# Zero products at the head of TensorE's queue, later fetches of two weight groups, and row maxima begun at another time

## The chip, the cores and the metric

The kernel runs on one core of one Trainium2 chip. The metric is the device time of one execution in microseconds (us): a median over runs, and beside it the time of one execution that the hardware profiler recorded. The engines are named as in the profile: PE is TensorE (PEld its weight loads), DVE is VectorE, ACT is ScalarE, POOL is GpSimd, and SP is the queue that only issues transfers.

## The reference, cut to what matters

Sequence length 2048, model width 448, 16 heads of 28, an MLP of width 1792, all in float32.

```
g = sigmoid((x * gate_w).sum(-1))
q, k, v = heads of x @ wqkv
a = softmax(q k^T * 28**-0.5) v, heads joined, @ wo
y = layernorm(x)
b = gelu(y @ w1 + b1) @ w2 + b2
out = g * a + (1 - g) * b
```

## The kernel before

Every operand of a large product is split into a rounded high part and a remainder, and three products are summed in PSUM (high by high, high by low, low by high). Sequence columns go in four chunks of 512.

The kernel has three stretches. In the first, **the head**, one weight block (`wq[0]`), chunk 0 of the transposed input (`xh[0]`, `xl[0]`), two more weight blocks (`wq[3]`, `wq[4]`) and chunks 1 and 2 are fetched through SP into eight buffers and split: the high part by ACT (`x_high`, L102, `mixed_high`, L91), the remainder of x by DVE (`x_low`, L105), that of weights by POOL (`mixed_low`, L95 and L96). `head_split` (L833) issues the splits of one load; the loop at L847 calls it for loads 0 to 10, so for chunk 0, the three weight blocks and chunk 1. Then three full-height accumulations of 11 products each run on PE (L862), one for each of the weight blocks 0, 3 and 4, in the banks 0, 1 and 2. `QK.close` copies a finished bank out (ACT, L282) and stores it in DRAM (`qk`, L286).

In the second stretch, **the strips**, PE's order is written by a planner (`Strips.run`). PE's rows are used as four strips of 32, on which four products run beside each other. The planner keeps a clock of its own, with assumed costs per operation, and issues instructions in the order in which that clock says that they can go: tiles of `QK` (queries and keys), `Val` (values), `Up` and `Down` (the MLP), all with matmuls at L472. Into free strip places it puts the row maxima: `RowMax.one` issues a product of one query tile (`qd`) by 512 keys (`kd`) at L198 and its DVE reduction at L200. There are 1024 of these; those left at the end of the strips are done in the third stretch. PE's own instruction order is what the planner wrote: an instruction that waits holds up all that follow it. Everything else (loads with their `after` times, splits, the loads of keys and queries for the row maxima) is a task with a due time on the planner's clock, and each engine's order is that in which the tasks fell due.

When the last key tile of group 0 is closed, four tasks load the keys and queries of the row maxima through POOL's queue (`rowmax.load_k`, L178; `rowmax.load_q`, L184), and `hot[j]` gives the time at which strip `j` may begin with them:

```
for j in range(4):
    st.at(now + 6.0 + 1.2 * j, lambda j=j: (rowmax.load_k(0, j, nc.gpsimd), ...), pool=1.1)
    st.hot[j] = now + 12.0 + 1.2 * j
```

The value weights `wv` (four loads of 230 KB, L551 on POOL) are due at 32 on that clock, the first ten `w1` blocks at 50. POOL also fetches eight pairs of untransposed input rows (`bxr`) for the layer norm's statistics (DVE, L129 and L130); a buffer is fetched again when its statistics are done.

In the third stretch, **the attention**, a turn makes the scores of 5 or 6 units (L1087), exponentials (ACT, L1090), and value products of whole batches of four units (L1098). While row maxima are owed, a turn has 5 units and up to 3 row maxima (`lone`); later turns have 6. There are 1024 units.

Of the kernel before, what the change touches and what calls it, by code (L numbers as in the profile page):

```python
# [7 lines left out]
F32 = mybir.dt.float32  # L8
F32R = mybir.dt.float32r
# [6 lines left out]
P = 128  # L16
# [6 lines left out]
CH = 512  # L23
# [7 lines left out]
NW = 10  # L31
# [4 lines left out]
def kernel(ctx: ExitStack, tc: tile.TileContext, xt, wqk, wv, wo, xk, w1, b1, w2, b2,  # L36
                          ident_d, sel_d, out):
    nc = tc.nc
# [35 lines left out]
    bk = banks.tile([P, 8, CH], F32, name="bk")  # L74
    ctx.enter_context(tc.manual_schedule())

    p0 = ExitStack()
    px = p0.enter_context(tc.tile_pool(name="px", bufs=1))
    pw = p0.enter_context(tc.tile_pool(name="pw", bufs=5))
    pr = p0.enter_context(tc.tile_pool(name="pr", bufs=1))  # L80
    po = p0.enter_context(tc.tile_pool(name="po", bufs=4))

    lasting = [raws.tile([P, CH], F32, name=f"raw{i}") for i in range(4)]
    passing = [pr.tile([P, CH], F32, name=f"first{i}") for i in range(4)]
    wq, xh, xl = {}, {}, {}

    def four(r):
        return r.rearrange("p (a b) -> p a b", b=P)
# [134 lines left out]
    rowmax = RowMax()  # L223
# [28 lines left out]
    class QK(Piece):  # L252
# [18 lines left out]
        def full(self):  # L271
            w, h, l = wq[self.i], xh[self.c], xl[self.c]
            r = slice(64, 128) if self.i % 2 else slice(0, 64)
            ops = []
            for t in range(3):
                ops += [(w[:, t], h[:, t]), (w[:, t], l[:, t])]
            ops += [(w[:, 3], h[:, 3]), (w[r, 3], l[r, 3])]
            return ops + [(w[:, 4 + t], h[:, t]) for t in range(3)]

        def close(self, st, now):  # L280
            t = po.tile([P, CH], F32, name="qo")
# [106 lines left out]
    class Strips:  # L388


        def __init__(self, tiles):
            self.tiles = tiles
            self.t = [0.0] * 4
            self.visit, self.held = [None] * 4, [None] * 4
            self.feed, self.stat = Feed(self, []), Feed(self, bxr)
            self.live = []
            self.free = {b: 0.0 for b in range(6)}
            self.rm = {6: 0.0, 7: 0.0}
            self.dve = self.act = self.pool = -6.0
            self.clock = self.dma = -6.0  # L400
            self.tasks = []
            self.count = 0
            self.hot = [1e9] * 4
            self.hready, self.yready, self.xready, self.wready, self.w1ready, self.w2ready = {}, {}, {}, {}, {}, {}
            self.vready = 1e9
            self.did = {}
            self.handed = 0

        def use(self, engine, start, cost):
            setattr(self, engine, max(getattr(self, engine), start) + cost)  # L410
# [169 lines left out]
    def want_wq(st, m, **kw):  # L580
        def then(slot, end):
            st.feed.back(slot, end)
            st.wready[m] = end

        def use(r):
            wq[m] = pw.tile([P, 7, P], F32R, name="wq")
            two(st, lambda: mixed_high(wq[m], r), lambda: mixed_low(wq[m], r, m % 2), "pool", 1.6, lambda end: then(r, end))

        st.feed.add(wqk[m], 256, use, **kw)
# [11 lines left out]
    def want_w1(st, f, **kw):  # L601
        def then(slot, end):
            st.feed.back(slot, end)
            st.w1ready[f] = end

        def use(r):
            if f >= NW and w1p[0] is mw0:
                st.later.append(lambda: use(r))
                return
            w1s[f] = w1p[0].tile([P, 7, P], F32R, name=f"w1f{f}")  # L610
            two(st, lambda: mixed_high(w1s[f], r), lambda: mixed_low(w1s[f], r, f % 2), "pool", 1.6, lambda end: then(r, end))

        st.feed.add(w1[f], 256, use, **kw)
# [84 lines left out]
    def done(st, x, now):  # L698
        n = st.did[type(x), x.c]
        if isinstance(x, QK):  # L700
            st.qks.add((x.c, x.i))
            for old, new in ((0, 2), (3, 6)):
                if new not in wq and new not in st.asked and all((c, old) in st.qks for c in range(NC)):
                    st.asked.add(new)
                    want_wq(st, new)
                    st.feed.queue.insert(0, st.feed.queue.pop())
                    st.clock = max(st.clock, now)
                    st.feed.pump()
            if not st.keyed and all((c, m) in st.qks for c in range(NC) for m in (3, 4)):
                st.keyed = True  # L710
                for j in range(4):
                    st.at(now + 6.0 + 1.2 * j, lambda j=j: (rowmax.load_k(0, j, nc.gpsimd), rowmax.load_q(0, j, nc.gpsimd)), pool=1.1)
                    st.at(now + 16.0 + j, lambda j=j: rowmax.load_q(1, j))
                    st.hot[j] = now + 12.0 + 1.2 * j
        elif isinstance(x, Val):
            st.vals += 1
            if st.vals == NT:
                enter_mlp(st, now)
        elif isinstance(x, Up) and n == NF:
            if x.c + 1 < NC:  # L720
                st.go.add(x.c + 1)
                st.clock = max(st.clock, now)
                split_y(st, x.c + 1)
            else:
                early(st, now)

    def enter_mlp(st, now):
        p0.close()
        w1p[0] = w2p[0] = m1.enter_context(tc.tile_pool(name="mw", bufs=1, reuse_waits="tile"))
        mhp.append(m1.enter_context(tc.tile_pool(name="mh", bufs=1, reuse_waits="tile")))  # L730
        hh.extend(mhp[0].tile([P, CH], F32R, name=f"hh{f}") for f in range(NF))
        hl.extend(mhp[0].tile([P, CH], F32R, name=f"hl{f}") for f in range(NF))
        assert not st.stat.out - NT // 2 and all(any(x is y for y in st.feed.slots) for x in passing)
        st.feed.slots = [x for x in st.feed.slots if not any(x is y for y in passing)]
        st.late = True
        st.clock = max(st.clock, now)
        for go in st.later:
            st.at(st.act + 0.6, go)
        for f in range(NF):
            want_w2(st, f)  # L740
        want_ln(st, 1)

    def schedule_head(st):
        st.asked = set()
        st.qks, st.keyed, st.vals = {(0, 0), (0, 3), (0, 4)}, False, 0
        st.xready[1] = st.xready[0] = 0.0
        st.wready.update({0: 0.0, 3: 0.0, 4: 0.0})
        st.late, st.later = False, []
        st.xs, st.wvn, st.stats, st.lns, st.go, st.yn = {}, 0, 0, {}, {0}, {}
        for t in range(4):  # L750
            want_x(st, 3, t)
        for m in (1, 5):
            want_wq(st, m, after=9.0)
        for t in range(4):
            want_wv(st, t, after=32.0)
        for f in range(NW):
            want_w1(st, f, after=50.0)
        st.feed.pump()
        for i in range(NT // 2):
            want_stats(st, i, after=22.0)  # L760
        st.stat.pump()
        st.at(49.0, lambda: nc.sync.dma_start(ones.rearrange("j (a b) -> (j a) b", b=4 * S // P), one_t))
        st.at(50.0, lambda: nc.sync.dma_start(b1s, b1))
        st.at(51.0, lambda: nc.sync.dma_start(sel, sel_d.rearrange("p (j x) -> p j x", x=32)[:, :, 0]))
        st.at(51.5, lambda: nc.sync.dma_start(ident, ident_d))
        st.at(52.0, lambda: nc.sync.dma_start(b2b, b2.partition_broadcast(P)))
# [65 lines left out]
    def head_split(i):  # L832
        key, r = load[i], slots[i % 8]  # L833
        if key[0] == "wq":
            wq[key[1]] = pw.tile([P, 7, P], F32R, name="wq")
            mixed_high(wq[key[1]], r)
            mixed_low(wq[key[1]], r, key[1] % 2)
        else:
            x_high(*key[1:], r)
            x_low(*key[1:], r)  # L840

    loads = [nc.gpsimd]
    strips = Strips([])
# [3 lines left out]
    for i, key in enumerate(load):  # L847
        r = slots[i % 8]
        if key[0] == "wq":
            nc.sync.dma_start(four(r), wqk[key[1]])  # L850
        else:
            nc.sync.dma_start(r, xt[key[2], :, key[1] * CH:(key[1] + 1) * CH])
        if 3 <= i < 14:
            head_split(i - 3)
    strips.feed.slots = slots[7:] + slots[:3]
    schedule_head(strips)
    for b, m in enumerate((0, 3, 4)):
        x = QK(0, m)
        x.bank = b
        ops = x.full()  # L860
        for i, (w, v) in enumerate(ops):
            nc.tensor.matmul(bk[:, b], w, v, start=(i == 0), stop=(i == len(ops) - 1), skip_group_check=True)  # L862
        x.close(strips, -2.4 * (2 - b))
    for i in range(11, len(load)):
        head_split(i)
        strips.use("act", 0.0, 0.65)
        strips.use("dve", 0.0, 0.75)
        strips.feed.back(slots[i % 8], strips.dve + 0.5)
    strips.xready[2] = strips.dve + 0.2
    for c, block in ((1, (3, 4, 0)), (2, (3, 4)), (3, (3, 4)), (2, (0,)), (3, (0,))):  # L870
# [307 lines left out]
```

## Time and profile before

| | us |
|---|---|
| median of 3 runs | 1104.21 |
| lowest and highest | 1100.46, 1105.54 |
| the profiled execution's own time | 1101.01 |
| its span | 1099.1 |
| first product of the strips (L472) | 18.28 from the span's start |
| first product of the attention | 454.72 |

Times in the text are from the span's start. The profiled execution lies 3.2 us under the median and 0.55 us over the lowest run; 1.9 us of it lie outside the span. In the timeline, a row gives the start, the time during which the engine was busy with the merged instructions, the engine, the line, the operation, its operands and the count, and in brackets how long the engine had been idle before, and what released it.

### The profile page before, as it was taken

What the parts mean: (1) busy time and instruction counts of PE and PEld (TensorE: products, weight loads), DVE (VectorE), ACT (ScalarE), POOL (GpSimd) and SP (SyncE); (2) the same over time, 40 slices, a digit from 0 to 9 for tenths busy, and PEclk for the clock granted to TensorE, in tenths of its full rate; (3) what the DMA queues carried; (4) which work ended last, traced back from release to release, by engine and by line L of the source; (5) the groups of instructions that cost most, each with busy time, mean ns of one, the idle gap of its engine ahead of it and who ended that gap; (6) DMA issues with size and microseconds to landing.
All of it is one profiled execution on the core that took longest, in us unless ns stands there. A gap on an engine that the chain in (4) does not pass through costs nothing.

```text
span 1099.1 us, 30449 instructions
## 1 busy us (share of the span) xinstructions
PE 1078.3 (98%) x13153; PEld 727.7 (66%) x13153; DVE 739.7 (67%) x1185; ACT 633.4 (58%) x666; POOL 362.2 (33%) x372
## 2 busy tenths in 40 slices
PE   8989999999999999999999999999999999999998
PEld 5979999999999999744444444444444443454555
DVE  4169999999999999766676775676676664310102
ACT  5324264133042141387787887887887888856672
POOL 3456477535244038321101101310011214434431
PEclk9989999999999999999999999999999999999999
DMA  6685633203000105310000001400002102010211
GB/s 230 203 252 172 212 101 98 92 12 103 36 11 11 37 12 126 111 51 23 20 11 20 24 21 37 104 16 19 16 23 56 48 18 54 24 52 28 69 53 59
DMA packets 47463, 73.15 MB, mean 67 GB/s; under 512 B 13633, under 2 KB 28609, under 8 KB 46417
## 3 DMA queue, kind: packets, MB, share of 16 engines
q1 hardware_dynamic: 33888, 39.11, 12.7%
q0 software_dynamic: 4800, 16.89, 5.6%
q10 hardware_dynamic: 8640, 15.21, 3.9%
q8 instruction: 103, 1.69, 0.7%
q14 instruction: 32, 0.25, 0.1%
HBM read 51.75 MB, written 19.31 MB: 65 GB/s over the span
## 4 chain that ended last, share of the span: by engine, by line
PE 91%; ACT 3%; DMA 2%; issue 1%; POOL 1%; DVE 1%; ACTq 0%; DVEq 0%; SPq 0%; POOLq 0%
PE bk L472 33%; PE bk L1098 21%; PE bk L1087 18%; PE bk L198 14%; ACT p L1090 3%; PE bk L936 1%; PE bk L937 1%; PE bk L938 1%; PE bk L862 1%; DMA qd<-qk 1%; DMA qk<-qo 1%; POOL w1f L95 0%; DVE mx L200 0%; DMA first<-in_xt 0%; PE bk L1114 0%
## 5 line engine op out<-in xcount | busy, mean ns | idle before, releaser
L200 DVE TENSOR_REDUCE mx<-bk 128x1 f32<-128x512 f32 x1024 | 672.1, 689 | 203.2 <-PE bk L198 167.8
L1090 ACT ACTIVATE p<-bk 128x1536 f32<-128x1536 f32 (+1 forms) x393 | 481.6, 1281 | 143.9 <-PE bk L1087 137.7
L198 PE MATMUL bk<-kd,qd 28*128 28x512 f32 x1024 | 447.0, 439 | 6.1 <-DMA qd<-qk 5.2
L198 PEld LDWEIGHTS bk<-kd,qd 28*128 28x128 f32 x1024 | 186.5, 183 | 193.4 <-DVE mx L200 123.5
L472 PE MATMUL bk<-yh,w1f 32*128 32x512 f32 x1568 | 190.2, 393 | 0.1
L472 PE MATMUL bk<-yl,w1f 32*128 32x512 f32 x784 | 165.1, 390 | 0.0
L472 PEld LDWEIGHTS bk<-yh,w1f 32*128 32x128 f32 x1568 | 152.2, 183 | 2.4 <-ACT gb L382 0.8
L472 PE MATMUL bk<-w2h,hh 32*128 32x448 f32 x896 | 141.5, 366 | 0.0
L472 PE MATMUL bk<-w2l,hh 32*128 32x448 f32 x896 | 140.5, 364 | 0.1
L1098 PE MATMUL bk<-p,va 128*32 128x512 f32 x1024 | 131.2, 602 | 0.0
L1098 PE MATMUL bk<-p,vb 128*32 128x512 f32 x1024 | 129.3, 601 | 0.0
L350 POOL TENSOR_TENSOR hl<-h,hh 128x512 fp32r<-128x512 f32 x56 | 72.4, 1306 | 127.5 <-ACT hh L343 76.2
L1087 PE MATMUL bk<-yh,ka 29*128 29x512 f32 x512 | 107.8, 484 | 0.4 <-ACT gb L382 0.4
L472 PEld LDWEIGHTS bk<-yl,w1f 32*128 32x128 f32 x784 | 106.9, 183 | 0.4
L794 POOL CAST yh<-yl 128x512 fp32r<-128x512 f32 x16 | 9.8, 611 | 290.0 <-DMA yl<-qk 180.6
L472 PEld LDWEIGHTS bk<-w2l,hh 32*128 32x128 f32 x896 | 103.0, 183 | 0.7 <-DVE w2l L152 0.4
L472 PEld LDWEIGHTS bk<-w2h,hh 32*128 32x128 f32 x896 | 102.2, 183 | 0.1
L1087 PE MATMUL bk<-yh,kb 29*128 29x512 f32 x512 | 97.5, 477 | 4.1 <-ACT p L1090 4.1
L472 PE MATMUL bk<-w2h,hl 32*128 32x448 f32 x896 | 93.0, 363 | 0.0
L1087 PE MATMUL bk<-yh,la 28*128 28x512 f32 x512 | 88.8, 393 | 0.0
L1087 PE MATMUL bk<-yl,ka 28*128 28x512 f32 x512 | 87.2, 409 | 0.0
L382 ACT ACTIVATE gb<-bk 128x448 f32<-128x448 f32 x16 | 8.7, 544 | 130.2 <-PE bk L472 125.9
(137 smaller groups left out, 1593.7 us busy)
## 6 DMA issues: line engine op xcount, KB each, us to landing
qk<-qo ACTq DMA_DIRECT2D x28, 256.0 KB
raw<-in_xt SPq DMA_DIRECT2D x17, 256.0 KB
vs<-vt ACTq DMA_DIRECT2D x16, 256.0 KB
rc<-rls SPq DMA_DIRECT2D x60, 64.0 KB
bxr<-in_xk POOLq DMA_DIRECT2D x8, 448.0 KB, 6.1
gbs<-gb ACTq DMA_DIRECT2D x16, 224.0 KB
acc<-gbs SPq DMA_DIRECT2D x16, 224.0 KB
out_y<-acc SPq DMA_DIRECT2D x16, 224.0 KB
```

What stands on the lines that cost most here:

```text
L198: nc.tensor.matmul(ps, self.qd[n % 2][r, i * P:(i + 1) * P], self.kd[r, k * 512:(k + 1) * 512], start=True, stop=True)
L200: nc.vector.reduce_max(self.mx[n % 2][:, j, i, k:k + 1], ps, axis=AX)
L350: nc.gpsimd.tensor_sub(hl[f], h, hh[f].bitcast(F32))
L472: mm = nc.tensor.matmul(bk[:, x.bank, :n], a, b, start=x.first, stop=(len(x.rem) == 1 and m == len(ops) - 1), skip_group_check=True)
L794: nc.gpsimd.tensor_copy(h, l.bitcast(F32))
L862: nc.tensor.matmul(bk[:, b], w, v, start=(i == 0), stop=(i == len(ops) - 1), skip_group_check=True)
L936: nc.tensor.matmul(po, h, woh[:, g], start=(g == 0), stop=False, skip_group_check=True)
L937: nc.tensor.matmul(po, h, wol[:, g], start=False, stop=False, skip_group_check=True)
L938: nc.tensor.matmul(po, l, woh[:, g], start=False, stop=(g == NG - 1), skip_group_check=True)
L1087: nc.tensor.matmul(bk[:, i], w[r, ks], q[r], start=(p == 0), stop=(p == 2), skip_group_check=True)
L1090: nc.scalar.activation(t[:, :count], bk[:, first:first + count], AF.Exp, scale=SCALE)
L1098: nc.tensor.matmul(bk[32 * j:32 * j + 32, 7], vg[n // NC][:, k, 32 * j:32 * j + 32], prob.pop(4 * b + j), start=(k == 0), stop=(k == NT - ...
```

## The change

It has four parts.

1. Before the head's products, 512 columns of `kd` are set to zero by DVE. PE multiplies these zeros into bank 7, which holds nothing yet: nine products ahead of the first real one and two more ahead of the products 3, 6 and 9 of the first block (`warm`). The first block now takes the low product of each part directly after the high ones; the other two blocks keep their order.
2. The value weights are due at 42 and the first `w1` blocks at 54 on the planner's clock.
3. The loads of the first keys begin 0.5 earlier after the last key tile's close, they are counted in the planner's model of the transfers, and `hot[j]` is the modelled landing plus 1.5.
4. The planner's clocks of the engines and of the transfers begin at -1 and not at -6; weight blocks have buffers of their own (block 2 in the place of 0, block 6 in that of 3); a late `w1` split waits for the moment at which the MLP's buffers are open.

```
+    PLACE = {2: 0, 6: 3}
...
-            self.dve = self.act = self.pool = -6.0
-            self.clock = self.dma = -6.0
+            self.dve = self.act = self.pool = -1.0
+            self.clock = self.dma = -1.0
...
+            if f >= NW and st.clock < st.opened:
+                st.at(st.opened, lambda: use(r))
+                return
...
+                def first(j):
+                    rowmax.load_k(0, j, nc.gpsimd)
+                    rowmax.load_q(0, j, nc.gpsimd)
+                    st.use("pool", st.clock, 1.1)
+                    st.hot[j] = st.get(st.pool, 290) + 1.5
+
                 for j in range(4):
-                    st.at(now + 6.0 + 1.2 * j, lambda j=j: (rowmax.load_k(0, j, nc.gpsimd), rowmax.load_q(0, j, nc.gpsimd)), pool=1.1)
+                    st.at(now + 5.5 + 1.2 * j, lambda j=j: first(j))
                     st.at(now + 16.0 + j, lambda j=j: rowmax.load_q(1, j))
-                    st.hot[j] = now + 12.0 + 1.2 * j
...
         for t in range(4):
-            want_wv(st, t, after=32.0)
+            want_wv(st, t, after=42.0)
         for f in range(NW):
-            want_w1(st, f, after=50.0)
+            want_w1(st, f, after=54.0)
...
         if 3 <= i < 14:
             head_split(i - 3)
+    nc.vector.memset(rowmax.kd[:, 0:CH].bitcast(F32), 0.0)
+    WARM = {0: 9, 3: 2, 6: 2, 9: 2}
+
+    def warm(n):
+        for _ in range(n):
+            nc.tensor.matmul(bk[:, 7], rowmax.kd[:, 0:P], rowmax.kd[:, 0:CH], start=True, stop=True, skip_group_check=True)
...
     for b, m in enumerate((0, 3, 4)):
         x = QK(0, m)
         x.bank = b
-        ops = x.full()
+        highs, lows = x.full()
+        if b == 0:
+            ops = sum((highs[t] + lows[t:t + 1] for t in range(4)), [])
+        else:
+            ops = sum(highs, []) + lows
         for i, (w, v) in enumerate(ops):
+            if b == 0 and i in WARM:
+                warm(WARM[i])
             nc.tensor.matmul(bk[:, b], w, v, start=(i == 0), stop=(i == len(ops) - 1), skip_group_check=True)
-        x.close(strips, -2.4 * (2 - b))
+        x.close(strips, -2.2 * (2 - b))
     for i in range(11, len(load)):
         head_split(i)
-        strips.use("act", 0.0, 0.65)
-        strips.use("dve", 0.0, 0.75)
+        strips.use("act", 1.0, 0.65)
+        strips.use("dve", 1.8, 0.75)
```

More of the change, by code (lines that the diff above doesn't have):

```diff
@@ L78 @@
     px = p0.enter_context(tc.tile_pool(name="px", bufs=1))
-    pw = p0.enter_context(tc.tile_pool(name="pw", bufs=5))
+    pw = p0.enter_context(tc.tile_pool(name="pw", bufs=1))
     pr = p0.enter_context(tc.tile_pool(name="pr", bufs=1))
@@ L273, in full @@
             r = slice(64, 128) if self.i % 2 else slice(0, 64)
[L274 to L278, printed above, removed]
+            highs = [[(w[:, t], h[:, t]), (w[:, t], l[:, t])] for t in range(3)]
+            highs.append([(w[:, 3], h[:, 3]), (w[r, 3], l[r, 3])])
+            return highs, [(w[:, 4 + t], h[:, t]) for t in range(3)]
         def close(self, st, now):
@@ L585, in use @@
         def use(r):
-            wq[m] = pw.tile([P, 7, P], F32R, name="wq")
+            wq[m] = pw.tile([P, 7, P], F32R, name=f"wq{PLACE.get(m, m)}")
             two(st, lambda: mixed_high(wq[m], r), lambda: mixed_low(wq[m], r, m % 2), "pool", 1.6, lambda end: then(r, end))
@@ L736, in enter_mlp @@
         st.clock = max(st.clock, now)
+        st.opened = st.act + 0.6
         for go in st.later:
-            st.at(st.act + 0.6, go)
+            st.at(st.opened, go)
         for f in range(NF):
@@ L834, in head_split @@
         if key[0] == "wq":
-            wq[key[1]] = pw.tile([P, 7, P], F32R, name="wq")
+            wq[key[1]] = pw.tile([P, 7, P], F32R, name=f"wq{key[1]}")
             mixed_high(wq[key[1]], r)
```

## The prediction

> **What bounds the kernel now.** I read the page's engine shares and chain first, then the list of who waited for whom on PE, then windows around the one long wait, then the timeline of single engines.
>
> ```profile
> PE 1078.3 (98%) x13153; PEld 727.7 (66%) x13153; DVE 739.7 (67%) x1185; ACT 633.4 (58%) x666; POOL 362.2 (33%) x372
> ...
> PE 91%; ACT 3%; DMA 2%; issue 1%; POOL 1%; DVE 1%; ACTq 0%; DVEq 0%; SPq 0%; POOLq 0%
> ```
>
> PE is busy for 98% of the span and makes 91% of the chain. So time is won or lost where PE stands still, where its clock is low, or where its strips are badly filled. PE's list of waits has one long entry behind the head:
>
> ```profile
> PE bk L198 <- DMA qd<-qk: 5.2, 1, 5.2
> ```
>
> (total, times, longest). Windows around it (length, then busy time of PE, PEld, DVE, ACT and POOL with counts, then granted clock, share of the DMA engines, GB/s):
>
> ```profile
> 56.90:62.24 5.34, 0.18 (x3) 0.03 (x2) 0.31 (x1) 0.46 (x1) 3.67 (x5) 0.90 0.95 254
> 62.24:68.04 5.80, 5.80 (x54) 5.07 (x58) 3.27 (x7) 1.55 (x4) 1.28 (x3) 0.50 0.51 150
> ```
>
> PE stands for 5.2 us, and the 5.80 us behind that are granted half the clock. The stop costs 5.2 us and half of 5.8 us, 2.9 us: 8.1 us together.
>
> The head, on PE's timeline:
>
> ```profile
> 9.25 0.79 PE L862 MATMUL bk<-xl,wq 64*128 64x512 f32 x1
> ...
> 12.70 0.63 PE L862 MATMUL bk<-xl,wq 128*128 128x512 f32 x1
> 13.12 0.54 PE L862 MATMUL bk<-xh,wq 128*128 128x512 f32 x1
> ...
> 15.51 0.39 PE L862 MATMUL bk<-xl,wq 128*128 128x512 f32 x1
> 15.74 0.40 PE L862 MATMUL bk<-xh,wq 128*128 128x512 f32 x1
> ...
> 16.66 0.39 PE L862 MATMUL bk<-xh,wq 128*128 128x512 f32 x1
> 16.98 0.50 PE L862 MATMUL bk<-xl,wq 64*128 64x512 f32 x1
> 17.40 0.95 PE L862 MATMUL bk<-xh,wq 128*128 128x512 f32 x3
> 18.28 0.50 PE L472 MATMUL bk<-xh,wq 32*128 32x512 f32 x3
> ```
>
> A product takes 0.42 us from start to start at first (12.70 to 13.12) and 0.23 us later (15.51 to 15.74). The half-height product costs its block 0.28 us more (0.32 and 0.42 us where two steps would be 0.46), and the passage to the strips 0.19 us (17.40 and three steps is 18.09; they begin at 18.28).
>
> **Part 1, the zeros: +11.1 us.** In the source the zeroing of `kd` stands behind the loop that issues the splits of chunk 1, and so it does in DVE's instruction order of the changed program: four small fills, four splits of chunk 0, four of chunk 1, then the zeroing, the thirteenth. PE's first instruction there is a zero product, and it waits for that thirteenth. Nothing of PE stands ahead of it, and all of PE's work stands behind it. DVE before:
>
> ```profile
> 0.84 0.11 DVE L63 MEMSET one_t<- 128x64 f32 x1
> ...
> 12.32 2.15 DVE L105 TENSOR_TENSOR xl<-first,xh 128x512 fp32r<-128x512 f32 x3
> ```
>
> The splits of chunk 1 end at 12.32 + 2.15 = 14.47, and nothing that they wait for comes from PE, so they end there in the changed kernel too. A fill of 128x512 isn't in the trace: at least the 0.11 us of a fill an eighth as long, at most the 0.72 us of a split of its size (2.15 / 3); I take 0.45, between them. PE begins at 15.0. I read this as in-order execution from the rows: the twelve earlier DVE instructions ran in program order. The Trainium skill (TensorE: Matmul & The Clock Gate, Part 1) says the same in so many words, that ACT and DVE are strict FIFO; by it the zeros can't come sooner, and it speaks against this change.
>
> At 15.0 everything that the three blocks read is split, so PE runs through 33 + 15 = 48 products without a wait, the first of them cold. Cold stretches in the trace: 5.8 us behind the stop, and about 4.2 us in the head (steady work from 9.25; the step is down by 13.4). I take 5.0: 11.8 products at 0.425. The other 36.2 at 0.23 are 8.3 us, three half-height products 0.8, the passage 0.2. The strips begin at 15.0 + 5.0 + 8.3 + 1.0 = 29.3 or 29.4, where they began at 18.28: **+11.1 us**. With 4.2 or 5.8 us cold it is 0.4 less or more, with the fill's ends 0.3, so +10.3 to +11.8. Nothing hides this: PE is the bound from there on. The same page (Part 1) has the clock released after about 3.4 us of steady work; that would be 0.8 us less. The trace has longer stretches, and they decide.
>
> ACT's queue has the three copies of finished banks ahead of chunk 2's splits, as before; it moves with PE, and chunk 1 keeps PE busy meanwhile.
>
> **Parts 2 and 3, the stop: -8.1 us.** The chain in order of time, then POOL's queue, then the first row maximum on PE:
>
> ```profile
> 44.32 5.86 DMA qk<-qo
> 53.98 8.12 DMA qd<-qk
> ```
>
> ```profile
> 50.23 0.58 POOL L178 DMA_DIRECT2D kd<-qk  x1
> ...
> 51.88 1.60 POOL L551 DMA_DIRECT2D first<-in_wv  x3
> ...
> 58.28 0.51 POOL L184 DMA_DIRECT2D qd<-qk  x1 [1.55 <-DMA first<-in_wv]
> ```
>
> ```profile
> 55.42 0.46 PE L198 MATMUL bk<-kd,qd 28*128 28x512 f32 x1
> ```
>
> The last key store (44.32) lands at 50.18, the first keys are asked for at 50.23, then come the value weights, and the second query load, issued at 53.98 behind them, takes 8.12 us. It lands at 62.10, and PE stands for it until 62.24. In the changed order all eight loads of keys and queries stand together on POOL, and the value weights behind two `bxr` fetches after them. The changed PE order has 671 strip products ahead of the first row maximum, before 604, which took 55.42 - 18.28 = 37.1 us. At that rate 671 take 41.3 us: the first row maximum comes at 29.4 + 41.3 = 70.7. The last key product has nearly the same place, so the store goes 26.0 us behind the strips' begin, at 55.4, and lands at 61.3. Eight issues of about 0.55 are 4.4 us. Even if the last of them takes the full 8.12 us it lands at 73.8; the first pair, at some 5 to 8 us, at 67 to 70. The order wants the second strip 1.2 us, the third and fourth some 6 and 7 us after the first. So no stop, or a short one, and with it goes the cold stretch: **-8.1 us** (ends -5 and -8.1).
>
> **Strip filling: -1.5 us.** The changed order has 530 row maxima ahead of the attention, before 542. Two windows of the strips:
>
> ```profile
> 140.00:200.00 60.00, 59.81 (x983) 55.79 (x976) 55.23 (x83) 30.78 (x53) 45.18 (x39) 1.00 0.37 107
> 200.00:454.70 254.70, 254.45 (x4411) 245.80 (x4403) 248.80 (x393) 67.89 (x109) 105.85 (x93) 1.00 0.17 48
> ```
>
> A product costs 254.7 / 4411 = 0.058 us, so twelve fewer save 0.7 us. From 140 to 200 it is 0.061 us: 983 x 0.0033 = 3.2 us of unfilled places around the first `Up` and `Down` tiles, which another order can fill or double. I take -0.8 of that, with ends of -3.2 and +3.2. Together -1.5.
>
> **Attention: +1.0 us.** By the program's order there are 159 turns of 5 units, 38 of 6 and one of 1; before 154, 42 and one of 2. The chain shows value batches at a fixed beat:
>
> ```profile
> 517.19 1.86 PE bk L1098 x16
> 528.88 1.85 PE bk L1098 x16
> ...
> 998.52 1.85 PE bk L1098 x16
> 1005.20 1.85 PE bk L1098 x16
> ```
>
> Four turns of 5 are 11.69 us (2.92 each), two turns of 6 are 6.68 us (3.34 each). 5 x 2.92 - 4 x 3.34 = +1.2, less a little for the shorter last turn: +1.0 (ends 0.4 and 2).
>
> **Part 4** only sets due times; its effect is in the counted order. Sum: +11.1 - 8.1 - 1.5 + 1.0 = **+2.5 us**, 1103.5 for an execution like the profiled one. That one lies 3.2 us under the median, so the forecast is 1104.2 + 2.5 = 1106.7 us.
>
> **Rivals.** *The zeros run during the first transfers, as the change means it* (zeroing ahead of the splits, PE warm by 9 us): the first block then ends with chunk 0's last split, near 9.3, and two blocks of 11 x 0.23 + 0.28 = 2.8 us end at about 15.2, so the head is 3 us shorter and the sum -3.1 - 8.1 - 1.5 + 1.0 = -11.7: 1092.5. DVE's order speaks against it: 4%.
>
> *The stop stays*: PE's order still wants a load that hasn't landed. Then the -8.1 is lost and the time is 1114.8, half of it with a stop too short to lower the clock. It decides from a first pair later than 70.7. For it: the DMA engines were 95% busy in that stretch. Against it: 920 KB less stand ahead. 8%.
>
> *The value weights come late*, and PE stops at its first value product instead; the mechanism that makes the kernel slower:
>
> ```profile
> 63.03 0.69 DVE L200 TENSOR_REDUCE mx<-bk 128x1 f32<-128x512 f32 x1 [5.82 <-PE bk L198]
> 63.64 0.62 DVE L129 BATCH_NORM_STATS2 stt<-bxr 128x6 f32<-128x448 f32 x1
> ```
>
> ```profile
> 67.64 2.08 POOL L114 TENSOR_TENSOR wvs<-first,wvs 128x450 fp32r<-128x450 f32 x2 [1.62 <-ACT wvs L110]
> ```
>
> ```profile
> 89.51 0.46 PE L472 MATMUL bk<-wvs,xh 32*128 32x450 f32 x2
> ```
>
> Before, the splits were done by 71, 18 us ahead of use. In the changed POOL order three of them stand behind a `bxr` fetch that waits for statistics, and these stand on DVE behind 13 row maxima: 70.7 + 13 x 0.69 + two statistics of at most 2.5 = 84.7, then 0.7 for the fetch and some 4 for three splits and an issue: 89.4. PE comes to its first value product after about as many products as before, at 89.5 + 11.1 - 8.1 - 1 = 91.5. It decides when POOL is 2 us later than that; each further us costs one, and over some 3 to 5 us the clock falls as well: 1109 to 1116, at the middle 1112. 14%.
>
> **How the numbers follow.** A measurement of this kernel can tell about 0.5%, 5.5 us, from no change. My case has 74%: +2.5 with ends from 1101 to 1112 by its terms and by the spread of the runs; 5% of it lie under -5.5 and 6% over +5.5, by the strip filling and a short wait, 63% between. With the first rival (4%) faster has 9%. The stop that stays (8%), 10 of the 14% of late value weights and those 6% make 24% slower; 67% are within. The range leaves out the first rival and the worst of the stops: 1098.5 to 1114.5.
>
> **What would show it.** Right: PE's first row a zero product near 15.0, waiting for DVE; the strips' begin near 29.4; no wait over 1 us at L199 and a granted clock of 1.00 from 50 to 80; the attention's begin 1 to 3 us later than 454.7. Wrong: a first zero product near 1 or 2 us; a wait on `qd`, `kd` or `wvs` of several us; an attention (454.7 to the end, 644 us) that is longer or shorter by over 2 us.

## The result, and the profile after

| | before | after |
|---|---|---|
| median, us | 1103.83 (4 runs) | 1112.80 (4 runs, 1111.18 to 1113.73) |
| the profiled execution's own time | 1101.01 | 1112.62 |
| its span | 1099.1 | 1110.5 |
| first product of the strips | 18.28 | 29.63 |
| first product of the attention | 454.82 | 464.66 |
| last product | 1093.61 | 1105.02 |

(The 454.72 given for the attention's begin before is that of a row maximum just ahead of its first product.) The changed kernel is slower: the ratio of the times is 1.0092, 95% interval 1.0070 to 1.0114. The forecast was +2.5 us, measured were +9.0 us by the medians and +11.4 us by the two spans (the profiled execution of before lies 2.8 us under its median, that of after 0.2 us). The busy times on the page of after:

```profile
PE 1078.6 (97%) x13168; PEld 727.9 (66%) x13168; DVE 737.4 (66%) x1186; ACT 634.6 (57%) x668; POOL 364.0 (33%) x372
```

PE is busy for 1078.6 us, where it was 1078.3, but the sum hides three differences: it is 1.5 us longer in the head (15 products of zeros), 2.8 us shorter in the strips and 1.6 us longer in the attention. The time in which PE stands grew from 20.8 us (1099.1 - 1078.3) to 31.9 us (1110.5 - 1078.6), and so nearly all of the 11.4 us is to be looked for in the list of PE's waits (total, times, longest):

```profile
PE bk L868 <- DVE kd L863: 14.7, 1, 14.7
...
PE bk L199 <- issue: 2.0, 1, 2.0
PE bk L1108 <- ACT gb L381: 1.8, 1, 1.8
PE bk L471 <- ACT hh L342: 1.3, 1, 1.3
...
PE bk L199 <- DVE mx L201: 0.8, 1, 0.8
PE bk L471 <- ACT gb L381: 0.5, 1, 0.5
PE bk L471 <- ACT qo L281: 0.4, 1, 0.4
```

The long wait for `qd` of before is gone; a wait of 14.7 us for the fill stands at the head, and behind it six of 0.4 to 2.0 us within the strips. PE's timeline of after (start, busy, engine, line, operation):

```profile
14.71 4.21 PE L868 MATMUL bk<-kd 128*128 128x512 f32 x9 [14.71 <-DVE kd L863]
...
20.00 0.64 PE L868 MATMUL bk<-kd 128*128 128x512 f32 x2
20.47 0.39 PE L883 MATMUL bk<-xh,wq 128*128 128x512 f32 x1
20.70 0.40 PE L883 MATMUL bk<-xl,wq 128*128 128x512 f32 x1
...
29.63 0.50 PE L471 MATMUL bk<-xh,wq 32*128 32x512 f32 x3
...
70.20 0.39 PE L199 MATMUL bk<-kd,qd 28*128 28x512 f32 x1
```

DVE's timeline shows the fill directly behind the splits of chunk 1:

```profile
11.97 2.15 DVE L106 TENSOR_TENSOR xl<-first,xh 128x512 fp32r<-128x512 f32 x3
14.18 0.48 DVE L863 MEMSET kd<- 128x512 f32 x1
```

The zeros come 14.71 us after the begin, when all inputs of the three blocks have landed and are split; steps of 0.23 us begin at 20.00; the strips begin at 29.63; the first row maximum has no bracket, so it waits for nothing. Windows of after (length, busy time of PE, PEld, DVE, ACT, POOL, granted clock, DMA share, GB/s):

```profile
276.14:278.15 2.01, 0.00 (x1) 0.03 (x2) 0.22 (x1) 0.00 (x0) 0.00 (x0) 1.00 1.01 181
279.41:282.82 3.41, 3.41 (x41) 3.41 (x37) 2.18 (x4) 0.00 (x0) 2.25 (x2) 0.50 0.29 96
...
463.73:470.56 6.83, 5.90 (x27) 4.07 (x31) 1.29 (x2) 2.91 (x3) 0.32 (x2) 0.50 0.74 210
```

and the one of before that answers to the last:

```profile
457.16:460.57 3.41, 3.41 (x11) 2.31 (x14) 1.15 (x2) 1.95 (x2) 0.00 (x0) 0.50 0.68 192
```

There is a new stop at 276, with the DMA engines full, and 3.41 us at half the clock from 279.41, 1.26 us behind its end. At the attention's begin the half clock lasts 6.83 us where it lasted 3.41.

In the experiments each ratio is to the kernel before on the same chip, whose median there was 1101.6 to 1103.3 us; so kernels of different chips are compared by their ratios. One execution of `e1_fill_first`, the profiled one, was granted 0.65 of the clock and took 1444.81 us; it is left out below, and the profile of that kernel is the one of `e5_fill_first_again`.

### The profile page after: what moved, and what is told of

Its sections match the earlier page's. It is cut to its first block, busy times and chain, and to the rows that moved or that the text cites. A ratio compares the mean times of both kernels' runs of the same rounds, so it can differ in the third digit from the quotient of the medians.

```text
span 1110.5 us, 30491 instructions
## 1 busy us (share of the span) xinstructions
PE 1078.6 (97%) x13168; PEld 727.9 (66%) x13168; DVE 737.4 (66%) x1186; ACT 634.6 (57%) x668; POOL 364.0 (33%) x372
## 4 chain that ended last, share of the span: by engine, by line
PE 92%; ACT 3%; DMA 2%; DVE 1%; issue 1%; POOL 0%; SPq 0%; DVEq 0%; ACTq 0%
PE bk L471 33%; PE bk L1119 21%; PE bk L1108 18%; PE bk L199 14%; ACT p L1111 2%; PE bk L957 1%; PE bk L958 1%; PE bk L959 1%; PE bk L883 1%; DMA qk<-qo 1%; DMA first<-in_xt 1%; DVE mx L201 1%; PE bk L868 1%; PE bk L1135 0%; POOL hl L349 0%
## 5 line engine op out<-in xcount | busy, mean ns | idle before, releaser
L199 PE MATMUL bk<-kd,qd 28*128 28x512 f32 x1024 | 446.3, 438 | 4.3 <-issue 2.0
L199 PEld LDWEIGHTS bk<-kd,qd 28*128 28x128 f32 x1024 | 186.5, 183 | 197.2 <-DVE mx L201 130.0
L471 PE MATMUL bk<-yh,w1f 32*128 32x512 f32 x1568 | 184.6, 393 | 0.5 <-ACT gb L381 0.5
L471 PE MATMUL bk<-yl,w1f 32*128 32x512 f32 x784 | 161.4, 393 | 0.0
L471 PE MATMUL bk<-w2h,hh 32*128 32x448 f32 x896 | 133.8, 367 | 1.3 <-ACT hh L342 1.3
L471 PE MATMUL bk<-w2l,hh 32*128 32x448 f32 x896 | 132.7, 364 | 0.0
L471 PEld LDWEIGHTS bk<-yl,w1f 32*128 32x128 f32 x784 | 103.5, 184 | 0.2
L471 PEld LDWEIGHTS bk<-w2h,hh 32*128 32x128 f32 x896 | 99.5, 184 | 1.8 <-ACT hh L342 1.7
L471 PEld LDWEIGHTS bk<-w2l,hh 32*128 32x128 f32 x896 | 100.0, 184 | 0.1
L471 PE MATMUL bk<-w2h,hl 32*128 32x448 f32 x896 | 88.4, 364 | 0.0
```

Source lines behind the costliest of these rows:

```text
L199: nc.tensor.matmul(ps, self.qd[n % 2][r, i * P:(i + 1) * P], self.kd[r, k * 512:(k + 1) * 512], start=True, stop=True)
L471: mm = nc.tensor.matmul(bk[:, x.bank, :n], a, b, start=x.first, stop=(len(x.rem) == 1 and m == len(ops) - 1), skip_group_check=True)
```

## Experiments

| kernel | median, us | ratio to before, 95% |
|---|---|---|
| changed kernel again (`e11_after_again`) | 1113.31 | 1.0091, 1.0066 to 1.0115 |
| zeros alone, fill late (`e3_zeros_alone`) | 1113.17 | 1.0097, 1.0082 to 1.0113 |
| change without zeros (`e2_no_zeros`) | 1099.61 | 0.9986, 0.9966 to 1.0006 |
| change, fill first (`e1_fill_first`) | 1098.29 | 0.9962, 0.9949 to 0.9975 |
| the same again (`e5_fill_first_again`) | 1100.62 | 0.9967, 0.9952 to 0.9982 |
| zeros alone, fill first (`e7_early_zeros_alone`) | 1101.85 | 0.9995, 0.9982 to 1.0008 |
| value weights later alone (`e6_values_later_alone`) | 1109.92 | 1.0072, 1.0052 to 1.0092 |
| change, last chunk's fetch later (`e9_after_x_later`) | 1110.49 | 1.0074, 1.0053 to 1.0095 |
| that, and copies by DVE (`e10_after_x_later_dve`) | 1110.04 | 1.0074, 1.0051 to 1.0096 |
| fill first, last chunk's fetch later (`e4_x_later`) | 1097.12 | 0.9963, 0.9944 to 0.9982 |
| that, and copies by DVE (`e8_best`) | 1097.80 | 0.9949, 0.9937 to 0.9961 |
| e4, and two more copy buffers (`e12_gb_in_h`) | 1097.19 | 0.9944, 0.9924 to 0.9965 |

**The head.** Four edits of the zeros. In the changed kernel the fill goes ahead of the loop of splits:

```
+    nc.vector.memset(rowmax.kd[:, 0:CH].bitcast(F32), 0.0)
     for i, key in enumerate(load):
...
-    nc.vector.memset(rowmax.kd[:, 0:CH].bitcast(F32), 0.0)
```

> The changed kernel with one line moved: kd is zeroed ahead of the loop that issues the splits, so the zero products need not wait for chunk 1. PE's order is that of the changed kernel to the instruction. The strips should begin near 15.2 us and not at 29.6, 14.4 us earlier. Theory A, the rest of the loss is in the new PE order (a 2.9 us wait of a row maximum for the second key group near 275 us, a later begin of the attention's first turn): both waits stay, the time is 1112.8 - 14.4 = 1098.4. Theory B, the rest of the loss comes from the late head, which sets all transfers against the strips: the waits go as well, the time is about 1091.

In the changed kernel, no fill and no zero products:

```
-    nc.vector.memset(rowmax.kd[:, 0:CH].bitcast(F32), 0.0)
...
-            if b == 0 and i in WARM:
-                warm(WARM[i])
```

> The changed kernel without the zeroing and without the zero products; all else stays, the new order of the first block too. The head should be that of before, strips from 18.3 us, 11.3 us earlier than in the changed kernel. Theory A (the new PE order holds the rest of the loss): 1112.8 - 11.3 = 1101.5, about 2 us better than before, with the wait for the second key group still there. Theory B (the late head holds it): 1094.

In the kernel before, part 1 of the change alone, with the fill where the change puts it:

```
+        highs, lows = x.full()
+        if b == 0:
+            ops = sum((highs[t] + lows[t:t + 1] for t in range(4)), [])
+        else:
+            ops = sum(highs, []) + lows
...
+            if b == 0 and i in WARM:
+                warm(WARM[i])
```

> The kernel before with part 1 alone: late zeroing, zero products, new order of the first block; strips, due times and the planner as before. The strips should begin at 29.6. Theory A: +11.3, 1115.1, the old 5 us stop for the first keys still there, no wait for the second key group. Theory B (a late head costs more than itself): about 1122, with a new wait later in the strips.

The late zeros alone make the kernel as slow as the whole change does (1.0097 against 1.0092), and without them, or with an early fill, it isn't slower (0.9986 and 0.9962). So the loss that the times show is the place of one fill on DVE's queue. What the other parts of the change bring together is small: some 0.3% with early zeros (0.9962 and 0.9967 against the 0.9995 of the early zeros alone, below), and nothing that can be told with late ones. In the profile of the zeros alone the strips begin at 29.86 and the old stop is still there, shorter:

```profile
PE bk L198 <- DMA qd<-qk: 4.0, 1, 4.0
```

It has neither the stop at L199 for the second key group nor the 1.8 us at the attention's begin. Both are there in the changed order with an early fill (1.8 and 1.8 us, `e5_fill_first_again`) and without zeros (2.4 and 1.8 us, `e2_no_zeros`). So they come with the new order on PE and not with the late head: theory A holds in all three (the 2.9 us of the first expectation are 2.0 in the list of after).

The first edit once more, for its profile:

> The kernel of e1_fill_first once more, for a profile at full clock (the first one was taken at a granted clock of 0.65, where products and transfers stand otherwise to each other). If the loads of input chunk 3 delay the second key group, its profile shows a wait of 2 to 3 us at L199 near 263 us and a half-clock stretch behind it, and the strips take 3 us longer than in e4_x_later (434.9 against 431.8 from their begin to the attention's first score product). If e4's gain came from elsewhere, there is no such wait. Time 1098.5; e4 was 1097.1.

and part 1 alone in the kernel before, with the fill ahead of the loop:

```
+    nc.vector.memset(rowmax.kd[:, 0:CH].bitcast(F32), 0.0)
     for i, key in enumerate(load):
```

> The kernel before with part 1 alone and the zeroing ahead of the splits: zero products while the first transfers run, as the change was meant; strips and due times as before. By e4_x_later's head (strips from 17.10, before 18.28) it gains 1.2 us, not the 3 us of my rival, because the inputs' splits and not the clock set the first block: 1100.4, which 3 rounds can hardly tell from 1101.6. If the head were bound by the clock alone, 1098.5. The old stop for the first keys stays.

PE's timeline of the changed kernel with the early fill:

```profile
1.63 3.81 PE L868 MATMUL bk<-kd 128*128 128x512 f32 x9 [1.63 <-DVE kd L855]
5.40 0.50 PE L883 MATMUL bk<-xh,wq 128*128 128x512 f32 x1
6.12 0.50 PE L883 MATMUL bk<-xl,wq 128*128 128x512 f32 x1 [0.23 <-DVE xl L106]
6.46 0.40 PE L883 MATMUL bk<-xh,wq 128*128 128x512 f32 x1
6.69 0.63 PE L868 MATMUL bk<-kd 128*128 128x512 f32 x2
...
17.10 0.50 PE L471 MATMUL bk<-xh,wq 32*128 32x512 f32 x3
```

and of part 1 alone with it:

```profile
8.35 0.49 PE L873 MATMUL bk<-xh,wq 128*128 128x512 f32 x1 [1.27 <-ACT xh L102]
9.07 0.63 PE L873 MATMUL bk<-xl,wq 128*128 128x512 f32 x1 [0.23 <-DVE xl L105]
9.50 0.63 PE L873 MATMUL bk<-xh,wq 128*128 128x512 f32 x1
...
19.63 0.50 PE L470 MATMUL bk<-xh,wq 32*128 32x512 f32 x3
```

Early zeros do bring the fast steps forward: from 6.46 to 6.69 a step takes 0.23 us, and the strips begin at 17.10, 1.2 us sooner than before. That is less than the 3 us of the prediction's first rival: the first block still waits for its splits, and six more zeros stand in it. In the second profile PE waits 1.27 us for a split of ACT's, which waits for a transfer, and behind that the steps are slow again (9.07 to 9.50 is 0.43 us), and the strips begin later than before. So the early zeros are worth little by themselves, as the ratio of 0.9995 says; this profiled execution was the slowest of its ten (1106.42), so its other stops aren't read.

**The stop at 276.** The rest of the change costs something that its gains hide. SP's queue of after, where the second group's keys and queries and the four loads of the last input chunk are issued:

```profile
269.83 0.38 SPq L179 DMA_DIRECT2D kd<-qk  x1
270.32 0.32 SPq L185 DMA_DIRECT2D qd<-qk  x1
270.74 1.27 SPq L179 DMA_DIRECT2D kd<-qk  x1
272.10 2.10 SPq L548 DMA_DIRECT2D raw<-in_xt  x4
275.80 0.54 SPq L220 DMA_DIRECT2D ms<-mt  x1
```

and of before:

```profile
261.28 0.39 SPq L178 DMA_DIRECT2D kd<-qk  x1
263.50 0.53 SPq L219 DMA_DIRECT2D ms<-mt  x1
264.97 2.70 SPq L549 DMA_DIRECT2D raw<-in_xt  x4
```

Before, 3.3 us lie between the end of the last key issue (261.67) and the first of the input's four 256 KB loads, after only 0.1 us. The profile names no releaser for PE's stop (`issue`) and has no landing of the key loads; that the stop waits for them is a guess, which the next edit tests. The edit moves those loads back, once with the early fill and once in the changed kernel as it is:

```
-                        st.at(end + 0.5, lambda: want_ln(st, c + 1))
+                        st.at(end + (12.5 if c == 2 else 0.5), lambda: want_ln(st, c + 1))
```

> As e1_fill_first, and the four loads of input chunk 3 for the MLP are asked for 12 us later, so that they don't stand right behind the loads of the second key group. If the wait near 275 us comes from these loads sharing the DMA engines with the keys, it goes, with its half-clock stretch: 3 to 4 us better than e1_fill_first. If the keys are simply asked for too late, the wait stays and the two kernels are equal within 1 us.

> The changed kernel as it is, with the fetch of the last input chunk for the layer norm 12 us later on the planner's clock. PE's, DVE's, ACT's and POOL's orders stay as they are, and on SP's queue the four loads of that chunk come behind one small store of maxima instead of ahead of it. Theory (the second key group's loads are slow because 1 MB of input is issued 0.1 us behind them): the 2.0 us wait at L199 near 276 shrinks below 0.5, the 3.41 us at half clock behind it go, the strips take 431 to 432 us instead of 435.0, and the time is 2.0 + 1.7 = 3.7 under the changed kernel's, about 1109 against 1112.8. Rival (the loads are late because they are issued late, at 269.8 and 270.3, whatever follows them): the wait stays, 1112 to 1114.

> The changed kernel again, for a comparison on one chip with the two kernels above: 1111 to 1114, with a wait of about 2 us at L199 in most executions.

In the second pair nothing differs but SP's queue, where the four loads stand behind one small store instead of ahead of it. SP's queue, then PE's waits and a window of that kernel:

```profile
270.90 1.25 SPq L179 DMA_DIRECT2D kd<-qk  x1
272.23 0.53 SPq L220 DMA_DIRECT2D ms<-mt  x1
280.76 1.78 SPq L548 DMA_DIRECT2D raw<-in_xt  x4
```

```profile
PE bk L1108 <- ACT gb L381: 1.8, 1, 1.8
PE bk L199 <- DVE mx L201: 1.4, 3, 0.8
```

```profile
276.00:284.00 8.00, 7.67 (x144) 7.29 (x142) 7.34 (x12) 0.00 (x0) 0.00 (x0) 1.00 0.26 85
```

The wait on `issue` is gone from the list, and the clock stays at 1.00. The last key load is issued 5.5 us before PE comes to the place of the stop (270.90 and 276.40), in after 5.4 us (270.74 and 276.14), so it isn't its issue that was late: the rival falls. The stop is in all four profiles at full clock of the new order without this edit (1.4 to 2.4 us) and in none of the five with it. From the strips' begin to the attention's first product it takes 431.2 us, in after 435.0, in its second profile 433.6 (there the stop was 1.44 us and didn't lower the clock). The medians are 2.8 us apart, in the direction expected, but their intervals overlap: shown by the profiles, not settled by the times. With the early fill the strips take 431.8 us with the later loads, 436.1 without, but the ratios are the same (0.9963 against 0.9962 and 0.9967); the 3 to 4 us that were expected aren't seen in the times.

**The attention's begin.** PE's 1.8 us wait there is for ACT's copy of a finished down tile. Two remedies were tried. The first lets DVE copy every other tile of the last chunk:

```
-            nc.scalar.activation(gb, bk[:, self.bank, :D], AF.Copy)
+            if self.c == NC - 1 and self.i % 2:
+                nc.vector.tensor_copy(gb, bk[:, self.bank, :D])
+            else:
+                nc.scalar.activation(gb, bk[:, self.bank, :D], AF.Copy)
```

> e4_x_later, and in the last chunk two of the four down tiles are copied out of PSUM by DVE and not by ACT. If the attention's first score product waits for ACT's chain of four copies and their stores (1.8 us in the changed kernel, with 6.8 us at half clock around it against 3.4 before), the wait falls under 1 us and the time to 1097.1 minus 1 to 2.5: 1095.4. If something else ends that wait last, nothing changes: 1097.1. Either way it should beat both kernels.

> The same, and DVE copies every other finished tile of the last column chunk's down tiles, which ACT alone copies in the changed kernel. Theory (the bunched copies at the attention's begin are a part of the loss): the 1.8 us wait of the first score product shrinks to about 1.1 as DVE takes its share, 0.5 to 1 us under the kernel without this edit: about 1108.3. Rival (what holds PE there is not the copy but the order): the same time as without the edit, and the half clock stays.

The wait falls to 1.1 us, but the time doesn't move by more than the noise (1110.04 and 1110.49 on one chip; ratios of 0.9949 and 0.9963 with the early fill): the last row maximum now waits 1.24 us for DVE where it waited 0.78. The remedy takes work from ACT, but ACT isn't short of time there; it waits, as its timeline of after shows:

```profile
461.42 0.54 ACT L381 ACTIVATE gb<-bk 128x448 f32<-128x448 f32 x1 [0.46 <-PE bk L471]
...
463.01 0.54 ACT L381 ACTIVATE gb<-bk 128x448 f32<-128x448 f32 x1 [1.05 <-DMA gbs<-gb]
```

The third copy waits 1.05 us for a store, because `gb` has two buffers. The second remedy gives the last two tiles the buffers of the up tiles, which are free by then:

```
-            gb = mhp[0].tile([P, D], F32, name="gb", bufs=2)
+            if self.c == NC - 1 and self.i > 1:
+                gb = mhp[0].tile([P, CH], F32, name="h", bufs=2)[:, :D]
+            else:
+                gb = mhp[0].tile([P, D], F32, name="gb", bufs=2)
```

> The kernel with the early fill and the later fetch of the last input chunk (e4_x_later), and the last two down tiles' copies go to two other buffers (those of the finished up tiles) instead of waiting for the stores of the two before. Theory (PE's 1.8 us wait at the first score product is ACT's third copy, which waits 1.05 us until the store of the first has read its buffer): the third and fourth copy come 1 us sooner, the wait falls to about 0.8, and if the stretch at half clock behind it shortens from 6.83 to 3.41 us another 1.5 us go: 1095.8 to 1096.5 as against 1097.1 without this edit, or 1094.5 with the shorter stretch. Rival (the wait is the bunching itself, four tiles that finish within 2.5 us): no change in the wait, 1097.

```profile
448.04 0.54 ACT L384 ACTIVATE h<-bk 128x448 f32<-128x448 f32 x1 [0.46 <-POOL wol L932]
```

The third copy starts 1.00 us behind the second instead of 1.59; PE's wait falls from 1.75 to 1.20 us and the half clock from 6.83 to 3.41 us. The attention takes 639.6 us from first to last product, without the edit 640.9. But the strips of this execution took 0.7 us longer (432.5 and 431.8), the wait that is left is longer than the 0.8 us expected, and the ratio is lower than that of `e4_x_later` by less than its interval: the mechanism is shown, its worth isn't. With 0.9944 it is the fastest version by ratio, some 6 us under the kernel before.

**The value weights by themselves.** In the kernel before, `after=32.0` becomes `after=42.0` and nothing else:

> The kernel before with one number changed: the value weights due at 42 and not at 32. The first row maximum keeps its place in PE's order (637 products ahead of it, as before). Theory K: the stop came from the value weights' 920 KB standing ahead of the second key and query load; then the stop shrinks from 5.2 us to under 2 us and the half-clock stretch goes: 1101.6 - 6 = 1095.6, changed by what the new order does later. Rival H: the row maxima were simply begun too early by the planner; then the stop stays at 4 us or more and the time is 1101 to 1102.

It is slower, 1.0072. The old stop falls from 5.2 to 0.9 us with the first row maximum at its old place (55.87, before 55.42), so theory K has the stop right and rival H falls; but its 1095.6 us don't come, because another stop appears, 45 us later. PE's waits, then ACT's timeline:

```profile
PE bk L472 <- ACT zall L312: 5.1, 1, 5.1
...
PE bk L198 <- DMA kd<-qk: 3.2, 1, 3.2
```

```profile
99.44 0.33 ACTq L315 DMA_DIRECT2D vs<-vt  x1
99.88 0.16 ACT L312 ACTIVATE zall<-bk 128x1 f32<-128x1 f32 x1
106.88 0.54 ACT L311 ACTIVATE vt<-bk 128x448 f32<-128x448 f32 x1 [6.84 <-DMA vs<-vt]
```

The fourth value tile's copy waits 6.84 us for a store out of one of three `vt` buffers, while four 256 KB loads that POOL issued at 98.87 are under way; PE waits behind ACT for the bank, and 6.83 us at half clock go with it. It looks like the stop at 276 in another place: a transfer that PE needs soon, with 1 MB issued beside it. No run moves these four loads alone, so that they are the cause isn't shown. The 3.2 us for `kd` at 702, with 13.65 us at half clock, are in this execution, the slowest of its four (1114.89); whether the others had it isn't known.

## Why the prediction fell short, step by step

| step | forecast, us | measured, us |
|---|---|---|
| zeros | +11.1 | +11.35 |
| the stop | -8.1 | -8.1 |
| strip filling | -1.5 | -1.6 |
| new waits in the strips and their clock | no term | +8.2 |
| attention | +1.0 | +1.6 |
| sum | +2.5 | +11.4 |

- **Zeros**: right to 0.3 us. DVE kept its program order, and the fill took 0.48 us (forecast 0.45), so PE began at 14.71 (15.0). The cold stretch was 5.3 us, 14.71 to 20.00 (5.0). The rule cited for this, strict order on DVE (the Trainium skill, TensorE: Matmul & The Clock Gate, Part 1), agrees; the 3.4 us that the page gives for the release doesn't show here. With early zeros, begun at 1.63, the first fast step came between 4.78 (`e5_fill_first_again`) and 7.34 (`e12_gb_in_h`), so the length of the cold stretch differs by some 2.6 us between executions, and that 5.0 came so near is in part luck.
- **The stop**: right. The first row maximum came at 70.20 (70.7) with no wait, and the value weights were ready: their first product at 91.63 (91.5) stood for nothing. Neither rival about these happened.
- **Strip filling**: this is the step that failed, not in what it counted but in what it was taken to be: all else that could change between the strips' begin and the attention. From 435.0 us in after go the six waits shown above, 2.01 + 1.77 + 1.28 + 0.78 + 0.39 + 0.50 = 6.73, and half of the 3.41 us of low clock behind the stop at 276, 1.7: 426.6. From 436.5 in before go the old stop's 8.1 and 0.27: 428.2. The difference of -1.6 is the filling, where -1.5 was forecast; it is a remainder, and how much of it each of the forecast's two parts (-0.7 and -0.8) gave isn't shown. The waits of the new order, 6.73 - 0.27 + 1.7 = +8.2, had no term. Most of that (6.8 us) are three places: the second group's turnover at 276 (2.0 and 1.7; gone when the input's loads move), ACT's copies at the attention's begin (1.8; the store of a two-buffer tile) and ACT's `hh` at 423 (1.3; not tried).
- **Attention**: inside its ends, the reason only in part. The attention of the changed order takes 639.2 and 639.6 us with 3.41 us at half clock at its begin (`e10_after_x_later_dve`, `e12_gb_in_h`), 640.3 to 640.9 with 6.83 (after and four others), 642.2 and 642.3 with 10.24 (`e11_after_again`, `e2_no_zeros`): some 1.4 us for each 3.41. Before took 638.8, with 3.41. So of the +1.6 the turns' recount is some 0.4 to 0.8 us, where 1.0 was forecast, and the clock, which had no term, gave the rest.

Of the signs that the prediction named, the head, the clock from 50 to 80 and `wvs` came out as the right ones; the attention's begin, forecast 1 to 3 us later, came 9.8 us later, and that was where to look.

The measured 1112.8 lies inside the range of 1098.5 to 1114.5, and that is luck: the case that was forecast ended at 1112, the range reached further up for a stop that stays and for late value weights, and neither happened. The likeliest case, less than 5.5 us from no change (67%), didn't come; of the 24% for slower, only the 6% for strip filling and a short wait are of the kind that did, and the waits in it had neither place nor size.

## What to carry to other kernels

A planner that moves one group of fetches moves the place of all later ones: after pricing the wait that goes, look on each queue for the next place where a small transfer that is wanted soon stands beside large ones, and at every tile with two or three buffers whose store must end before its next copy. A warm-up is worth something only if its own operand is ready first: one fill behind a loop of splits cost 11 us; ahead of it the same zeros let the strips begin 1.2 us sooner in one profile and 1.4 us later in another, and the times show no gain. A new order needs a term of its own for the waits that it makes: here they cost 8.2 us, as much as the stop that the order removed.

## What the runs showed of the hardware

- Stretches at half clock last 3.41, 6.83 (both in after), 10.24 (`e11_after_again`) or 13.65 us (`e6_values_later_alone`): multiples of 3.41, but for the one at the end of each execution. Their begins lie on the same grid: 279.41 and 463.73 in after are 184.32 us apart, 54 times 3.413; 61.21 and 457.15 in before 395.94 us, 116 times. The Trainium skill (TensorE: Matmul & The Clock Gate, Part 1) has a free-running window of 3413 ns, which agrees; by it about a whole idle window lowers the clock, and here less was enough.
- At the second group's turnover stops of 2.01 us (after) and 1.8 us (early fill) cost 3.41 us at half clock, stops of 1.44 us (after again) and 2.42 us (without zeros) none. The windows of the grid that hold them, in after, after again and without zeros, tell more (where the clock doesn't fall near the stop, the edges are counted back from its next fall, at 465.08 and at 455.23):

```profile
276.00:279.41 3.41, 1.40 (x28) 1.27 (x28) 1.12 (x3) 0.00 (x0) 0.00 (x0) 1.00 0.99 210
...
277.34:280.75 3.41, 1.97 (x37) 1.59 (x34) 1.67 (x4) 0.00 (x0) 0.00 (x0) 1.00 1.00 215
...
267.50:270.91 3.41, 1.74 (x32) 1.73 (x36) 1.24 (x2) 0.00 (x0) 0.00 (x0) 1.00 0.94 196
```

  PE stands for 2.01, 1.44 and 1.67 us of these windows (length less busy time), and for 1.80 us of that of the early fill (264.24 to 267.65): the 2.42 us lie across an edge of the grid, 0.75 us on one side and 1.67 on the other. All four fit if at this place it counts how much of a stop lies in one window, with a limit between 1.67 and 1.80 us. It is no limit for all places: 0.70 us in one window were enough at the attention's begin in before (453.74 to 457.15), and 1.50 us in the head of the early zeros alone (5.88 to 9.29); why there isn't shown.
- The granted clock in the profile's windows doesn't show the cold start: this row of after reads 1.00 while the products went 0.42 us apart.

```profile
14.71:20.00 5.29, 5.29 (x13) 4.13 (x13) 0.00 (x0) 0.00 (x0) 0.24 (x1) 1.00 0.48 172
```

- Products of zeros warm the clock: in `e5_fill_first_again` the steps of the nine zero products, before which PE had run nothing, fall from 0.43 us to 0.26 us with the ninth (4.78 to 5.04).
